# Column order batch by batch, and the even table one window earlier, in a DFT and squared-ReLU FFN kernel

## Chip, cores and metric

One NeuronCore of a Trainium2 chip. The metric is the device time of one execution in microseconds (us); less is better. The program is one core's alone, and there is no collective in it.

## What is computed

```
X = np.fft.fft(x, axis=1); X = np.fft.fft(X, axis=2)     # x: (8, 3008, 256) f32
t = X.real.reshape(8*3008, 256)
h = np.maximum(t @ w_in, 0.0)                            # w_in: (256, 2048)
out = h * h @ w_out                                      # w_out: (2048, 256), out: (24064, 256) f32
```

The kernel works in float16 with float32 accumulation in PSUM.

## The kernel before

**Columns.** A sequence row k of a batch and its mirror 3008 - k have transforms that differ only in the sign of one part. So the kernel works on *columns*: one column is the cosine part (`zc`) and the sine part (`zs`) of one row k, and it yields two output rows, "plus" and "minus". There are 1505 columns per batch, 12040 in all. A batch's columns come in two *units*: the odd unit (e = 0) with 752 columns, the even unit (e = 1) with 753. In each unit the first half of the columns is copied out of PSUM by ScalarE (L487) and the second half is made by VectorE from the same two accumulations (`minus`, L494).

**Order of the columns.** `units` (L86) lists the units in the order of their columns: before the change odd 0, odd 1, even 0, even 1, then odd i, even i for i = 2 to 7. (Numbers here are places in the order of work; batch 0 of the input is worked last.) The columns are cut into 25 *windows* (L73 to L78): w0 has 240 columns, w1 512, w2 and w3 376 each, w4 512, w5 448, then 512 each and 360 at the end. Unit odd 0 fills w0 and w1 exactly, odd 1 fills w2 and w3 exactly, even 0 begins at w4.

**What each window does** (L640 to L726). For each of 8 steps s, a window makes 256 of the 2048 hidden features for its columns: `pq` (L684, L685: four matmuls into PSUM, cosine and sine part), `square` with sign 0 (a ReLU by ScalarE from PSUM, L694, and a square by VectorE, L696, into `h2`), then `others(s)`, then `turn` (L690: two matmuls that turn plus into minus), and `square` with sign 1. `others(s)` holds all side work: first the list `at[s]`, then a share of the second FFN matmul of the *previous* window (L596, half groups of 8 matmuls, and their evacuation by ScalarE, L611, and stores on SP's queue, L576), then `post[s]`, then a share of the matmuls that make the columns of a later unit (`z_steps`, L478). In w0, w1 and w4 two steps are taken together (`ng` = 2): both `pq`, both squares, `others` of the first, both turns, both squares, `others` of the second.

**Buffers that tie the engines.** The PSUM tile `ph` has 2 buffers and `h1`, between ReLU and square, has 3. So TensorE can be at most two steps ahead of the ReLUs, and ScalarE at most three squares ahead of VectorE. Each engine works its queue strictly in the order of the program.

**Making a unit's columns.** For an odd unit `z_steps` issues 12 matmuls of 376 columns against the odd sine and cosine tables and the folded batch `od`. For an even unit it issues 20 matmuls of 188, 94 and 95 columns against the even tables `cos1`, `sin1` and the tiles `xt`, `yt`, `spn`. Between the first and the second half of each part ScalarE copies PSUM to `es` (L483). A unit that begins in window w+1 is made in window w (`need`), spread over steps `lo` to `hi` (L705 to L709), all at step 6 if `lo, hi = 6, 7`.

**Folding a batch** (`fold_steps`, L334). `d_even` (L348 to L350), `n_cos` (L358), `d_odd` (L353), `n_sin` (L361) and `odds` (L368) are VectorE work on the loaded batch `xo`; `nyq` (L373 to L375) is two tiny matmuls and a copy. `d_odd` also issues the load of the next batch, three to six DMAs on POOL's queue (L125, L130). `even` (L379) makes `ev` and writes it to a scratch in DRAM by a DMA of POOL's queue (L381); `back` reads it in four pieces, two by plain DMA (L389) and two by indirect DMA (L391), all on POOL's queue. `late` is four VectorE operations that read these pieces: two `fold8` (L404), two `fold16` (L415); behind the last come four tiny copies on POOL (`nyq8`, L421 to L423).

**The even table** (`table_steps(1)`): `freq` (L222, three operations), `args` (L232, two), `turns` (L236), `mods` (L242, two), `absm` (L245) and `weigh` (L265, four) on VectorE, `sins` (L248) and `coss` (L252) on ScalarE.

**The schedule before.** Ahead of w0: the odd table, odd half of fold 0, `gh` for all 2048 features, unit odd 0, then its two `minus` parts and `gh_turn(1)` to `gh_turn(3)` on VectorE (L543, L544, L558). In w0: `even` and `back` of batch 0 at step 2. In w1: fold 1 in steps 0 to 5 and unit odd 1 at step 6. In w2: `even` of batch 1, the even table, `late` of batch 0, `back` of batch 1. In w3: unit even 0. In w4: `late` of batch 1 in steps 0 to 3 and unit even 1 from step 4. From w5 on: fold 2, and so on in a steady pattern, a batch every three windows.

Of the kernel before, what the change touches and what calls it, by code (L numbers as in the profile page):

```python
# [19 lines left out]
def rev_dim(ap, i):  # L20

    dims = [list(d) for d in ap.ap]
    step, cnt = dims[i]
    dims[i] = [-step, cnt]
    return bass.AP(tensor=ap.tensor, offset=ap.offset + step * (cnt - 1), ap=dims)
# [3 lines left out]
def kernel(  # L29
# [15 lines left out]
    B, S, D = x.shape  # L45
    _, F = moe_w_in.shape
# [34 lines left out]
    def win_of(col):  # L81
        return max(w for w in range(NW) if wins[w][0] <= col) if col < TOT else NW


    bs = list(range(1, B)) + [0]
    units = [(0, 0), (1, 0), (0, 1), (1, 1)] + [(i, e) for i in range(2, B) for e in range(2)]  # L86
    runs = []
    col_of = {}
    g = 0
# [63 lines left out]
    def iota(shape, pattern, base, mult, name):  # L153
        t = const.tile(shape, I32, name=name)
        nc.gpsimd.iota(t, pattern=pattern, base=base, channel_multiplier=mult)
        return t
# [125 lines left out]
    at = const.tile([P, 2, P + 1], F32, name="at")  # L282
# [163 lines left out]
    def gh_turn(cc):  # L446
        f0 = cc * 512
        nc.vector.tensor_scalar(out=gh[:, 2, f0 : f0 + 512], in0=gh[:, 1, f0 : f0 + 512], scalar1=turn2[:, 0:1], scalar2=None, op0=ALU.mult)
# [3 lines left out]
    def zwin(w):  # L452
        if w not in zc:
            zc[w] = zp.tile([P, WN], F16, name="zc", tag="zc")
            zs[w] = zp.tile([P, WN], F16, name="zs", tag="zs")
        return zc[w], zs[w]
# [67 lines left out]
    def run(*jobs):  # L524
        for j in jobs:
            j()

    f0s = fold_steps(0)
    z0 = z_steps(need[0][0], late=True)
# [10 lines left out]
    gh_turn(0)  # L540
    gh3()
    run(*z0(1, 1))
    run(*z0(0, 2))  # L543
    run(*z0(1, 2))  # L544
    evec_i = iota([P, 2], [[1, 2]], 0, 2, "evec_i")

    evec = small([P, 2], "evec")
# [7 lines left out]
    nc.gpsimd.tensor_tensor(wge, wge, wg2, op=ALU.add)  # L555
    nc.gpsimd.tensor_scalar(out=wg2, in0=evec, scalar1=0.0, scalar2=-0.5, op0=ALU.is_equal, op1=ALU.mult)
    nc.gpsimd.tensor_tensor(wge, wge, wg2, op=ALU.add)
    for cc in range(1, F // 512):  # L558
        gh_turn(cc)

    def store(osb, p0, g0, m, minus, eng=nc.sync):

# [62 lines left out]
    def spread(jobs, i, n):  # L625
        return jobs[len(jobs) * i // n : len(jobs) * (i + 1) // n]

    folds = {0: f0s}

    def fold_jobs(i):  # L630
        f = folds[i] = fold_steps(i)
        return [f["d_even"], f["n_cos"], f["d_odd"], f["n_sin"], f["odds"], f["nyq"], f["even"], f["back"]]

    fold_at, late_at = {}, {}
    for i in range(2, B):
        fold_at[win_of(col_of[i, 0]) - 2] = i
        late_at[win_of(col_of[i, 1]) - 2] = i
    NST = NFC // 2
    old = None
    for w in range(NW):  # L640
        g0, wn = wins[w]
        h2 = h2p.tile([P, NFC, 2 * WN], F16, name="h2", tag="h2")
        zcw, zsw = zwin(w)

        lo, hi = 0, NST - 1
        at = [[] for _ in range(NST)]
        post = [[] for _ in range(NST)]
        if w == 0:
            at[2] = [f0s["even"], f0s["back"]]
        elif w == 1:  # L650
            fj = fold_jobs(1)
            at = [[f] for f in fj[0:5]] + [[], [], []]
            post[5] = fj[5:6]
            lo, hi = 6, 7
        elif w == 2:
            te = table_steps(1)
            at = [[folds[1]["even"], lambda: te["freq"](), lambda: te["args"](0)], [lambda: te["turns"](0)], [lambda: te["mods"](0)],
                  [lambda: te["absm"](0)], [lambda: te["sins"](0)], [lambda: te["coss"](0)], [], [lambda: te["weigh"]()]]
            for st in range(4):
                at[st + 3] = at[st + 3] + f0s["late"][st : st + 1]  # L660
            at[7].append(folds[1]["back"])
        elif w in fold_at:
            fj = fold_jobs(fold_at[w])
            at = [[f] for f in fj[0:5]] + [[], fj[6:7], fj[7:8]]
            post[5] = fj[5:6]
        elif w == win_of(col_of[1, 1]) - 1:
            for st in range(4):
                at[st] = folds[1]["late"][st : st + 1]
            lo = 4
        if w in late_at:  # L670
            for st in range(4):
                at[st + 2] = at[st + 2] + folds[late_at[w]]["late"][st : st + 1]
        zj, zl = [], []
        for u in need[w + 1]:
            zu = z_steps(u)
            zj += [(zu, 0, 0), (zu, 1, 0), (zu, 0, 1), (zu, 1, 1)]
        f2 = ffn2_steps(*old) if old else []
        phs = {}

        def pq(s):  # L680
            ph = phs[s] = ps_h.tile([P, 2, 512], F32, name="ph", tag="psh")
            for a in range(2):
                f0 = (2 * s + a) * P
                nc.tensor.matmul(ph[:, a, 0:wn], gh[:, 0, f0 : f0 + P], zcw[:, 0:wn], start=True, stop=False)  # L684
                nc.tensor.matmul(ph[:, a, 0:wn], gh[:, 1, f0 : f0 + P], zsw[:, 0:wn], start=False, stop=True)  # L685

        def turn(s):
            for a in range(2):
                f0 = (2 * s + a) * P
                nc.tensor.matmul(phs[s][:, a, 0:wn], gh[:, 2, f0 : f0 + P], zsw[:, 0:wn], start=False, stop=True, skip_group_check=True)  # L690

        def square(s, sg):
            h1 = h1p.tile([P, 2, 512], F16, name="h1", tag="h1")
            nc.scalar.activation(h1[:, :, 0:wn], phs[s][:, :, 0:wn], AF.Relu)  # L694
            hv = rev_dim(h1[:, :, 0:wn], 2) if sg else h1[:, :, 0:wn]
            nc.vector.tensor_tensor(h2[:, 2 * s : 2 * s + 2, sg * wn : (sg + 1) * wn], hv, hv, op=ALU.mult)  # L696

        def others(s):
            for j in at[s]:
                j()  # L700
            for j in spread(f2, s, NST):
                j()
            for j in post[s]:
                j()
            if s == lo:  # L705
                zl[:] = [j for zu, part, h in zj for j in zu(part, h)]
            if s >= lo:
                for j in spread(zl, s - lo, hi - lo) if s < hi else []:
                    j()  # L709


        ng = 2 if w == 0 or wins[w - 1][1] < 384 < wn else 1
        for s0 in range(0, NST, ng):
            ss = range(s0, s0 + ng)
            for s in ss:
                pq(s)
            for s in ss:
                square(s, 0)
            others(s0)
            for s in ss:  # L720
                turn(s)
            for s in ss:
                square(s, 1)
            for s in ss[1:]:
                others(s)
        old = (w, h2)  # L726
# [32 lines left out]
```

## Time and profile before

| what | us |
|---|---|
| median of 3 runs (634.8 to 634.96) | 634.92 |
| the profiled execution | 633.9 |
| its span, first to last instruction | 632.0 |
| TensorE busy | 615.9 |
| ScalarE busy | 457.4 |
| VectorE busy | 369.5 |
| POOL busy | 76.5 |

The page divides one profiled execution by engine, line and tile. "PE" is TensorE, "DVE" VectorE, "ACT" ScalarE, "POOL" GpSimd, "SP" the engine whose queue issues the stores. A line such as "L694" is a line of the kernel. An instruction's shown duration reaches into that of the next one where they are pipelined: eight matmuls of 256 columns at L596 are shown with 1.04 us, but the next work on TensorE begins 0.87 us after they began. What an instruction takes from its engine is the distance to the next start.

TensorE's first matmul of w0 starts at 21.73 us of the span, that of w1 at 31.68, of w2 at 53.20, of w3 at 74.81, of w4 at 94.54, of w5 at 116.98.

### The profile page before, as it was taken

How to read it: one execution, taken by the hardware profiler on the slowest of the kernel's cores; microseconds unless marked ns; L12 is line 12 of the kernel's file. 1: busy time of each engine (PE TensorE's matmuls, PEld its weight loads, DVE VectorE, ACT ScalarE, POOL GpSimd, SP SyncE). 2: the span in 40 equal slices, each digit the busy share in tenths (PEclk: the TensorE clock that was granted, in tenths of full speed). 3: DMA queues.
4: the chain of work that ended last, by engine and by line, in shares of the span. 5: the costliest groups of instructions: out<-in, count | busy, mean ns of one | idle time of the engine just before them, and what ended most of it. 6: DMA issues, size and time to landing. Idle time of an engine off the chain costs nothing.

```text
span 632.0 us, 11586 instructions
## 1 busy us (share of the span) xinstructions
PE 615.9 (97%) x4548; PEld 439.1 (69%) x4548; DVE 369.5 (58%) x604; ACT 457.4 (72%) x610; POOL 76.5 (12%) x125
## 2 busy tenths in 40 slices
PE   5899999999999999999999999999999999999997
PEld 2457776776777767767777677777677776777786
DVE  7887656765457557645576455854557555454430
ACT  7787778777777677767777777777777777777662
POOL 5352200022002200220011100030000200000000
PEclk9999999999999999999999999999999999999999
DMA  8936211172112711631127211262111311111112
GB/s 146 211 82 127 85 34 34 50 164 78 36 43 58 184 46 42 144 97 35 51 44 160 74 52 39 59 151 73 40 31 55 111 34 47 38 46 35 49 54 65
DMA packets 36525, 47.52 MB, mean 75 GB/s; under 512 B 4216, under 2 KB 30328, under 8 KB 36472
## 3 DMA queue, kind: packets, MB, share of 16 engines
q0 software_dynamic: 9344, 22.14, 17.6%
q1 hardware_dynamic: 26899, 24.44, 12.7%
q8 instruction: 35, 0.57, 0.4%
q10 hardware_dynamic: 228, 0.21, 0.1%
q14 instruction: 19, 0.15, 0.1%
HBM read 33.63 MB, written 27.84 MB: 97 GB/s over the span
## 4 chain that ended last, share of the span: by engine, by line
PE 93%; DVE 3%; ACT 2%; issue 1%; POOL 0%; ACTq 0%; POOLq 0%; DVEq 0%
PE po L596 51%; PE ph L684 12%; PE ph L685 12%; PE ph L690 12%; PE pz L478 4%; ACT h L694 1%; PE pw L301 1%; DVE h L696 1%; PE pg L436 0%; ACT cos L259 0%; DVE fe L349 0%; DVE fo L353 0%; ACT sin L248 0%; ACT gh L440 0%; DVE od L368 0%
## 5 line engine op out<-in xcount | busy, mean ns | idle before, releaser
L694 ACT ACTIVATE h<-ph 128x1024 f16<-128x1024 f32 (+4 forms) x400 | 368.4, 974 | 80.0 <-PE ph L690 72.1
L696 DVE TENSOR_TENSOR h<-h 128x1024 f16<-128x1024 f16 (+4 forms) x400 | 262.4, 660 | 231.6 <-ACT h L694 228.2
L596 PE MATMUL po<-wout,h 128*128 128x256 f16 (+1 forms) x3024 | 361.6, 273 | 0.0
L596 PEld LDWEIGHTS <-h 128*128 128x128 f16 (+1 forms) x3024 | 296.8, 98 | 71.3
L684 PE MATMUL ph<-zc,gh 128*128 128x512 f16 (+4 forms) x400 | 145.9, 366 | 1.1 <-ACT h L694 0.8
L685 PE MATMUL ph<-zs,gh 128*128 128x512 f16 (+4 forms) x400 | 145.9, 366 | 0.4 <-ACT zs L487 0.4
L690 PE MATMUL ph<-zs,gh 128*128 128x512 f16 (+4 forms) x400 | 112.8, 366 | 2.0 <-ACT h L694 1.5
L611 ACT ACTIVATE osb<-po 128x512 f32<-128x512 f32 (+3 forms) x95 | 54.9, 582 | 57.4 <-PE po L596 52.4
L685 PEld LDWEIGHTS <-gh 128*128 128x128 f16 x400 | 39.1, 98 | 43.8 <-issue 2.5
L684 PEld LDWEIGHTS <-gh 128*128 128x128 f16 x400 | 39.0, 98 | 41.8 <-issue 0.5
L690 PEld LDWEIGHTS <-gh 128*128 128x128 f16 x400 | 37.2, 97 | 12.7 <-issue 4.3
L421 POOL COPY xt<-xt 128x2 f16<-128x2 f16 x16 | 2.5, 186 | 173.2 <-DVE xt L404 173.2
L130 POOL DMA_INDIRECT xo<-in_x_dram,idx_r x15 | 22.1, 1471 | 4.6 <-issue 4.6
L125 POOL DMA_DIRECT2D xo<-in_x_dram x8 | 6.0, 751 | 109.8 <-DVE fo L353 109.8
L483 ACT ACTIVATE es<-pz 128x376 f32<-128x376 f32 (+1 forms) x32 | 15.4, 481 | 5.3 <-PE pz L478 5.2
L391 POOL DMA_INDIRECT rb<-scr,idx_r x16 | 18.5, 1158 | 4.9 <-issue 4.9
L487 ACT ACTIVATE zs<-pz 128x376 f16<-128x376 f32 (+23 forms) x27 | 8.5, 358 | 9.9 <-PE pz L478 9.9
L349 DVE TENSOR_TENSOR fe<-xo 128x3072 f16<-128x3072 f16 x8 | 14.3, 1786 | 1.6 <-DMA xo<-in_x_dram,idx_r 1.3
L353 DVE TENSOR_TENSOR fo<-xo 128x3072 f16<-128x3072 f16 x8 | 14.2, 1779 | 0.0
L494 DVE SCALAR_TENSOR_TENSOR zc<-es,pz 128x376 f16<-128x376 f32 (+20 forms) x26 | 9.4, 392 | 7.2 <-ACT zc L487 7.0
L301 PE MATMUL pw<-spn 128*128 128x384 f16 x30 | 8.2, 448 | 5.2 <-DVE spn L290 5.2
L389 POOL DMA_DIRECT2D rb<-scr x16 | 8.8, 551 | 33.4 <-DMA scr<-ev 33.0
(106 smaller groups left out, 220.4 us busy)
## 6 DMA issues: line engine op xcount, KB each, us to landing
out_dram<-osb SPq DMA_DIRECT2D x77, 128.0 KB
xo<-in_x_dram POOLq DMA_DIRECT2D x7, 768.0 KB, 7.0
scr<-ev POOLq DMA_DIRECT2D x8, 390.0 KB, 4.4
rb<-scr POOLq DMA_DIRECT2D x16, 130.0 KB, 5.1
out_dram<-osb SPq DMA_DIRECT2D x12, 94.0 KB
w<-in_moe_w_in_dram POOLq DMA_DIRECT2D x2, 512.0 KB, 10.0
wout<-in_moe_w_out_dram POOLq DMA_DIRECT2D x1, 1024.0 KB, 14.5
out_dram<-osb SPq DMA_DIRECT2D x8, 75.0 KB
```

What stands on the lines that cost most here:

```text
L130: nc.gpsimd.indirect_dma_start(out=flat(q), out_offset=None, in_=bass.AP(tensor=x.tensor, offset=0, ap=[[XW, B * S * D // XW], [1, XW]]), ...
L301: nc.tensor.matmul(pw[:, 0 : 3 * P], spn[:, 0, 0, :], spn.rearrange("p c r d -> p (c r d)")[:, 0 : 3 * P], start=True, stop=True)
L391: nc.gpsimd.indirect_dma_start(out=rb[:, q].rearrange("p r d -> p (r d)"), out_offset=None, in_=bass.AP(tensor=src.tensor, offset=src.offs ...
L478: nc.tensor.matmul(ps[:, o0:o1], lhs, tab, start=(h == 0 and k == 0), stop=last, skip_group_check=True)
L483: nc.scalar.activation(es[:, 0:n], ps[:, 0:n], AF.Copy, bias=0.0, scale=1.0)
L596: nc.tensor.matmul(po[0:m, j * D : (j + 1) * D], h2[:, fc, q : q + m], wout16[:, fc, :], start=(fc == 0), stop=(fc == NFC - 1))
L611: nc.scalar.activation(osb[0:mm].rearrange("p s d -> p (s d)")[:, lo:hi], po[0:mm, lo:hi], AF.Copy, bias=0.0, scale=HS * HS)
L684: nc.tensor.matmul(ph[:, a, 0:wn], gh[:, 0, f0 : f0 + P], zcw[:, 0:wn], start=True, stop=False)
L685: nc.tensor.matmul(ph[:, a, 0:wn], gh[:, 1, f0 : f0 + P], zsw[:, 0:wn], start=False, stop=True)
L690: nc.tensor.matmul(phs[s][:, a, 0:wn], gh[:, 2, f0 : f0 + P], zsw[:, 0:wn], start=False, stop=True, skip_group_check=True)
L694: nc.scalar.activation(h1[:, :, 0:wn], phs[s][:, :, 0:wn], AF.Relu)
L696: nc.vector.tensor_tensor(h2[:, 2 * s : 2 * s + 2, sg * wn : (sg + 1) * wn], hv, hv, op=ALU.mult)
```

## The change

The order of the units becomes odd 0, even 0, odd 1, even 1, odd 2 and so on, so even 0 takes columns 752 to 1504 (w2, w3 and one column of w4), and odd 1 columns 1505 to 2256 (w4, w5). With it the side work of the first windows is moved: the even table and `late` of batch 0 go from w2 to w1, unit even 0 is made at step 6 of w1, fold 1 goes from w1 to w2 (with `even` and `back` at steps 6 and 7), unit odd 1 from w1 to w3, `late` of batch 1 from w4 to steps 4 to 7 of w3, and unit even 1 is spread over all of w4. The three `gh_turn` and the two `minus` of unit odd 0 go from ahead of w0 into its steps 0, 2 and 4. No operation of the table, the folds or the FFN is added or taken away.

```diff
-    units = [(0, 0), (1, 0), (0, 1), (1, 1)] + [(i, e) for i in range(2, B) for e in range(2)]
+    units = [(i, e) for i in range(B) for e in range(2)]
...
     run(*z0(1, 1))
-    run(*z0(0, 2))
-    run(*z0(1, 2))
...
-    for cc in range(1, F // 512):
-        gh_turn(cc)
...
-    for i in range(2, B):
+    for i in range(1, B):
         fold_at[win_of(col_of[i, 0]) - 2] = i
         late_at[win_of(col_of[i, 1]) - 2] = i
...
         if w == 0:
-            at[2] = [f0s["even"], f0s["back"]]
+            at[0] = [lambda: gh_turn(1)]
+            at[2] = [lambda: gh_turn(2), f0s["even"], f0s["back"]]
+            at[4] = [lambda: gh_turn(3)] + z0(0, 2) + z0(1, 2)
         elif w == 1:
-            fj = fold_jobs(1)
-            at = [[f] for f in fj[0:5]] + [[], [], []]
-            post[5] = fj[5:6]
+            te = table_steps(1)
+            fl = f0s["late"]
+            at = [[lambda: te["freq"](), lambda: te["args"](0)], [lambda: te["turns"](0), lambda: te["mods"](0)], [lambda: te["absm"](0), lambda: te["sins"](0)],
+                  [lambda: te["coss"](0), fl[0]], [lambda: te["weigh"](), fl[1]], fl[2:4], [], []]
             lo, hi = 6, 7
-        elif w == 2:
-            te = table_steps(1)
-            at = [[folds[1]["even"], lambda: te["freq"](), lambda: te["args"](0)], [lambda: te["turns"](0)], [lambda: te["mods"](0)],
-                  [lambda: te["absm"](0)], [lambda: te["sins"](0)], [lambda: te["coss"](0)], [], [lambda: te["weigh"]()]]
-            for st in range(4):
-                at[st + 3] = at[st + 3] + f0s["late"][st : st + 1]
-            at[7].append(folds[1]["back"])
         elif w in fold_at:
             fj = fold_jobs(fold_at[w])
             at = [[f] for f in fj[0:5]] + [[], fj[6:7], fj[7:8]]
             post[5] = fj[5:6]
-        elif w == win_of(col_of[1, 1]) - 1:
-            for st in range(4):
-                at[st] = folds[1]["late"][st : st + 1]
-            lo = 4
-        if w in late_at:
+        if w in late_at:
+
             for st in range(4):
-                at[st + 2] = at[st + 2] + folds[late_at[w]]["late"][st : st + 1]
+                at[st + (4 if w == 3 else 2)] += folds[late_at[w]]["late"][st : st + 1]
```

## The prediction

> **What bounds the kernel now.** I read the page's busy shares first, then busy time by window, then the chain of waits through w1, then the timelines of the engines there.
>
> ```profile
> span 632.0 us, 11586 instructions
> PE 615.9 (97%) x4548; PEld 439.1 (69%) x4548; DVE 369.5 (58%) x604; ACT 457.4 (72%) x610; POOL 76.5 (12%) x125
> ```
>
> TensorE is busy all the time but 16 us. The windows (stretch, length, then busy time per engine) say where:
>
> ```profile
> 21.70:31.68 9.98, 7.46 (x51) 4.61 (x49) 8.78 (x22) 8.58 (x18) 2.18 (x8) 1.00 1.04 216
> 31.68:53.20 21.52, 19.95 (x127) 12.25 (x127) 17.08 (x27) 17.69 (x22) 11.66 (x7) 1.00 0.55 97
> 53.20:74.81 21.61, 21.61 (x178) 17.23 (x176) 15.73 (x34) 15.57 (x24) 2.90 (x8) 1.00 0.29 87
> 74.81:94.54 19.73, 19.66 (x167) 15.61 (x164) 10.51 (x23) 15.10 (x24) 1.66 (x2) 1.00 0.20 61
> 94.54:116.98 22.44, 22.19 (x166) 15.45 (x164) 13.88 (x24) 19.16 (x27) 0.70 (x4) 1.00 0.11 37
> ```
>
> w0 (first line) is bound by ScalarE and VectorE, TensorE idles 2.5 us. w1 idles 1.6 us of TensorE. w2 and w3 are bound by TensorE outright. The columns behind w4 keep their order and their work, so all that can change lies between 21.7 and 117 us. In w1 the chain of waits runs through fold 1 on VectorE:
>
> ```profile
> 35.56 1.79 DVE fe L349
> ...
> 38.63 0.88 DVE ab L358
> ...
> 40.72 1.70 DVE fo L353
> ...
> 43.60 0.88 DVE ab L361
> 44.49 1.20 DVE h L696 x2
> 45.69 0.90 DVE od L368
> 46.59 0.05 issue
> 46.63 0.18 PE py L373
> ```
>
> The squares queue between the folds, and `pq` of step 6 (46.70) stands behind `py`, which waits for `od`. Without any wait it would start at 31.68 + 3 pairs of steps x 4.34 (per pair 12 matmuls of 512 columns at 0.216 and two half groups of 8 at 0.872) = 44.70. So fold 1 costs w1 2.0 us, and that is what moving it could give back.
>
> **Method.** I walk the three queues by hand through w0 to w4, with starts to the next start from the timelines: ReLU 0.52 (240 columns), 0.92 (512), 0.69 (376); square 0.39, 0.60, 0.47; 0.2 from a matmul's issue end to ScalarE, 0.1 from ScalarE to VectorE or TensorE. For the kernel before this ends w1 at 53.11 (trace 53.20) and w4 at 116.64 (116.98): 0.1 per window is its error where it is applied to known work.
>
> **w0: +0.4.** Two `minus` (0.45 each) and three `gh_turn` (0.30 each) stand ahead of the first square now, and ScalarE pays for it once:
>
> ```profile
> 24.81 1.03 ACT L694 ACTIVATE h<-ph 128x480 f16<-128x480 f32 x2 [0.36 <-DVE h L696]
> ```
>
> That wait goes. But at step 4 the block `gh_turn(3)` and both `minus`, 0.30 + 2 x 0.48 = 1.26, stands between squares, and the ReLU of step 7 needs the `h1` buffer of the square behind it: a wait of 0.63. At step 2 `gh_turn(2)` goes ahead of `even` (0.89): 1.19 between squares, a wait of 0.39 where `even` alone made 0.09. Sum -0.54 (0.36 in the trace) + 0.63 + 0.30 = +0.39. Bounds: -0.36 if VectorE catches up, +0.6 with the trace's 0.36. I take +0.39. `even` itself starts where it did (26.9), since it follows the square of step 3.
>
> **w1: -0.48.** Out go fold 1 (VectorE 2.0 + 0.88 + 1.70 + 0.88 + 0.89 + 0.1 = 6.45) and 12 matmuls of 0.158. In come the table and `late` 0: VectorE 0.42 + 0.66 + 0.46 + 1.04 + 0.46 + 0.97 for the table, 2 x 0.61 + 2 x 0.34 for `late`, 5.9 in all, in smaller lumps. But ScalarE gets two operations that fold 1 did not have:
>
> ```profile
> 65.73 0.84 ACT L248 ACTIVATE sin<-m 128x754 f16<-128x754 f32 x1
> 68.28 0.93 ACT L252 ACTIVATE cos<-t,halfpi 128x754 f16<-128x754 f32 x1
> ```
>
> In w2 they lie beside 1.75 us of second FFN matmuls per step; in w1 a pair of steps gives TensorE 4.34 and ScalarE 4 x 0.92 + 0.5 (evacuation, every second pair) = 4.18 already. With 1.6 more in the second pair, ScalarE needs 5.8. Walked: `pq` of steps 2 and 3 from 36.4; `sins` waits for `mods` until 39.55; the ReLU of step 2, sign 1, ends at 41.3, so `pq` of step 4 waits 0.63; `coss` and the evacuation push the ReLU of step 4 to 43.5, so `turn` of steps 4 and 5 waits 0.52 and 0.49. `pq` of step 6 then starts at 46.73, the old 46.70: 1.64 of the 2.0 is spent again, the rest is w0's +0.39.
>
> The columns of even 0 are 20 short matmuls, 1.12 us of TensorE (0.08 per 188 columns, 0.04 per 94), against 1.90:
>
> ```profile
> 49.30 0.64 PE L478 MATMUL pz<-cos,od 128*128 128x376 f16 x3
> 49.77 0.64 PE L478 MATMUL pz<-sin,od 128*128 128x376 f16 x3
> 50.51 0.64 PE L478 MATMUL pz<-cos,od 128*128 128x376 f16 x3
> 50.99 0.64 PE L478 MATMUL pz<-sin,od 128*128 128x376 f16 x3
> ```
>
> All stand at step 6, so this gains nothing: TensorE waits for `es` (0.48 each) before the second halves, and after them ScalarE must make `zc`, `zs` (two spans each now, 0.18 for the one-column span) before the last ReLUs, for which w2's first `pq` waits until 53.02. `nyq8` on POOL follows the last `fold16` (49.5) by 0.45 as at 71.76 to 72.63, so `spn` is 0.15 late for its matmuls, inside the wait for `es`. w1 ends 0.1 earlier than before; less w0's +0.39 its own share is -0.48. Bounds: +1.3 (the whole of `sins` and `coss`, 1.77, on top of my -0.48), -2.0 (no wait at all).
>
> **w2: +0.07, w4: 0.** Fold 1 in w2 is laid out as fold 2 is from 119.4 on, where TensorE showed 10.00 of 10 us busy. It brings the load of batch 2 (POOL's queue, issued near 61 instead of 42.7; first read at 119.4, so its 7 to 11 us of landing are covered). Behind it on POOL's queue are the scratch write and four reads of batch 1; `even` 1 at 71.2, scratch landed 4 to 7.2 later, four issues 3.7, landing 3.8: 83 to 86. `late` 1 asks at 86.5; VectorE has 9 us idle in w3, and three squares of play. I charge nothing; uncovered it would cost up to 1. Four more stores in w0 to w7 (91 for 87) go to SP, whose 424 us of waiting for `osb` cover them.
>
> **w3: +0.53.** It gets the 12 long matmuls for the 20 short ones: +0.78 of TensorE work in a window where TensorE is busy 19.66 of 19.73. The small gaps before `turn` that the short ones leave take up 0.25. This is the work that w1 could not use.
>
> **Sum:** +0.39 - 0.48 + 0.07 + 0.53 = +0.5. The profiled execution becomes 633.9 + 0.5 = 634.4; the median stands 1.02 above it, so 635.4.
>
> **Rivals.** (A) *The even pieces come too late for w1.* `fold8` asks near 42.9 instead of 63.95; VectorE, ScalarE and TensorE would wait behind it. From the walk, a landing after 44.75 moves the end one for one. Before, the last piece was issued here:
>
> ```profile
> 34.34 1.05 POOL L391 DMA_INDIRECT rb<-scr,idx_r  x1 [0.30 <-issue]
> 35.69 2.50 POOL L391 DMA_INDIRECT rb<-scr,idx_r  x1 [0.30 <-issue]
> ...
> 43.79 4.84 POOL L130 DMA_INDIRECT xo<-in_x_dram,idx_r  x1 [0.30 <-issue]
> ```
>
> With 3.6 to 5.9 from issue to landing it landed by 39.3 to 41.6: three us of play. But an indirect issue took 4.84 beside fold 1's VectorE work. Two of these: 34.34 + 4.84 + 0.30 + 4.84 + 2.8 (shortest landing) = 47.1, which is 2.4 too late: 635.4 + 2.4 = 637.8. For it: the 2.50 beside `fe`, and squares run on. Against: the two `fe`, `fo` of 1.7 us are no longer there.
>
> The Trainium skill (DMA: Bandwidth & Descriptors, SWDGE vs HWDGE vs iDMA) says that GpSimd writes such descriptors into rings in SBUF and that VectorE shuts it out during its two-port modes. By that rule the table's float32 operations (L232, L236, L245) could hold these issues as `fe` may have done, and the time would be A's 637.8. The trace shows none of them beside an indirect DMA; the plain issue beside L222 and L232, at 57.02, took 0.75 where 0.61 is the median.
>
> (B) *w1 truly gains.* If `sins` and `coss` fit between ReLUs, `pq` of step 6 starts near 44.7: -2.0 in w1, and -0.36 in w0, against +0.53: -1.8, 633.1. For it: ScalarE idles 3.8 of 21.5 us in w1. Against: its idle time lies in waits for TensorE, with only two `ph` buffers to run ahead in. (C) *The moves do nothing*: table and even pieces are ready earlier, but ScalarE's chain sets the end of w1 as before (-0.1 with w0), and the 0.78 in w3 lies in gaps: 634.92 - 0.1 = 634.8. Against: w3 shows 0.07 of idle TensorE.
>
> **Chances.** What a measurement of this kernel can tell from no change is about 0.2%, 1.27 us. Forecast with C, within that: 0.69; own range 634.3 (w0's waits at -0.36, w1 0.35 better) to 636.2 (w0 at +0.6, w1 0.6 worse, a third of the way to its bound). A: 0.13, slower. The forecast with w0 and w1 at their worse bounds, +0.2 and +1.77: 637.4, slower, 0.09. B: 0.09, faster. Range 633.8 to 637.3: most of A, of the worst bounds and of B lies outside or at its ends, under 0.2 in all.
>
> **What would show it.** ScalarE's wait for a square at 24.8 gone, and new ones near 28 and 31; w1 starting near 32.0, `sins` near 39.6, `pq` of step 6 near 46.7, w2 near 53.0; w3 about 20.2 long; no DMA wait ahead of L404. Wrong if L404 waits for `rb`, if `pq` of step 6 comes before 45.5, or if a window from w5 on changes its length by more than 0.2.

## The result, and the profile after

The changed kernel took 635.68 us (median of 22 runs) against 634.07 us for the kernel before on the same chips: ratio 1.0025, 95% interval 1.0016 to 1.0034, some 1.6 us slower. In a second series, beside the experiments below, the ratio was 1.0017 (1.0007 to 1.0028). So it is slower, by about as much as the 0.2% that the prediction called its limit of sight, and inside the stated range; the forecast was +0.5 us. Both medians of "before" lie below the 634.92 that the prediction started from, which were three runs; the ratios compare runs of the same chips.

The profiled execution took 635.0 us with a span of 633.1 us (633.9 and 632.0 before). The windows again, first the changed kernel's w0 to w4 (stretch, length, then busy time of TensorE, its weight loads, VectorE, ScalarE and POOL):

```profile
21.56:31.67 10.11, 7.37 (x51) 4.61 (x48) 8.63 (x22) 8.52 (x18) 2.32 (x8) 1.00 1.01 212
31.67:54.17 22.50, 19.58 (x133) 12.37 (x133) 17.25 (x38) 18.83 (x26) 6.77 (x8) 1.00 0.13 37
54.17:75.83 21.66, 21.66 (x180) 17.27 (x178) 16.63 (x26) 14.04 (x22) 3.60 (x4) 1.00 0.58 129
75.83:96.09 20.26, 20.18 (x158) 15.46 (x156) 11.87 (x24) 15.14 (x24) 3.47 (x6) 1.00 0.25 76
96.09:118.52 22.43, 22.18 (x167) 15.45 (x164) 11.97 (x20) 19.38 (x27) 0.39 (x2) 1.00 0.11 33
```

| window | before, us | forecast change | measured change |
|---|---|---|---|
| w0 | 9.95 | +0.39 | +0.16 |
| w1 | 21.52 | -0.48 | +0.98 |
| w2 | 21.61 | +0.07 | +0.05 |
| w3 | 19.73 | +0.53 | +0.53 |
| w4 | 22.44 | 0 | -0.01 |
| sum | 95.25 | +0.51 | +1.71 |

w0 began 0.17 us earlier in this execution, which is chance (it began at 22.05 in the next run of the same kernel), so w5 begins 1.54 us later than before (118.52 against 116.98), and TensorE's last long row of matmuls likewise (618.35 against 616.81). The span grew by 1.1 only: what lies behind TensorE's last matmul, the last stores and the end of the program, took 0.4 us less. No run shows why.

Only w1 is far off. TensorE's waits in w1, by engine and line waited for (total, times, longest), first before:

```profile
PE py L373 <- DVE od L368: 1.0, 1, 1.0
PE ph L690 <- ACT h L694: 0.5, 1, 0.5
```

and after:

```profile
PE pz L478 <- POOL xt L421: 1.0, 1, 1.0
PE ph L673 <- ACT h L683: 1.0, 1, 1.0
PE ph L679 <- ACT h L683: 0.6, 2, 0.3
PE pz L478 <- ACT es L483: 0.3, 1, 0.3
```

The wait for fold 1 is gone, and the ScalarE waits came at the three places that the walk had named. The first line is new: the columns of even 0 wait for the four tiny POOL copies of `nyq8`. The timelines of the changed kernel show why (start, duration, engine, line; "x2" merges two instructions). POOL:

```profile
47.81 3.19 POOL L421 COPY xt<-xt 128x2 f16<-128x2 f16 x2 [11.14 <-DVE xt L404]
50.94 0.18 POOL L422 COPY spn<-yt 128x2 f16<-128x2 f16 x1
```

and VectorE beside it:

```profile
47.05 0.69 DVE L404 TENSOR_TENSOR xt<-rb 128x1040 f16<-128x1040 f16 x1
47.66 1.29 DVE L685 TENSOR_TENSOR h<-h 128x1024 f16<-128x1024 f16 x2
48.86 0.77 DVE L415 TENSOR_TENSOR yt<-xt 128x520 f16<-128x520 f16 x2
49.54 1.29 DVE L685 TENSOR_TENSOR h<-h 128x1024 f16<-128x1024 f16 x2
```

A copy of two elements per partition, 0.19 us at the median of its 16 instances (0.18 before, 0.19 at most), took 3.07 us here, the first of the two merged in that line. It begins under a square and ends as the sixth VectorE operation of an unbroken row ends (49.54 + 1.29 = 50.83). All six have two inputs in SBUF. The matmul that reads `xt` starts at 50.94, 0.99 late, and the `es` behind it adds 0.32.

### The profile page after: what moved, and what is told of

Its sections match the earlier page's. It is cut to its first block, busy times and chain, and to the rows that moved or that the text cites. A ratio compares the mean times of both kernels' runs of the same rounds, so it can differ in the third digit from the quotient of the medians.

```text
span 633.1 us, 11600 instructions
## 1 busy us (share of the span) xinstructions
PE 616.1 (97%) x4548; PEld 439.0 (69%) x4548; DVE 369.7 (58%) x606; ACT 457.1 (72%) x612; POOL 73.9 (12%) x125
## 4 chain that ended last, share of the span: by engine, by line
PE 91%; ACT 3%; DVE 2%; POOL 1%; DMA 1%; issue 1%; ACTq 0%; POOLq 0%; DVEq 0%
PE po L592 51%; PE ph L679 12%; PE ph L673 12%; PE ph L674 12%; PE pz L478 4%; ACT h L683 2%; DMA w<-in_moe_w_in_dram 1%; DVE h L685 1%; POOL xt L421 0%; PE pg L436 0%; POOL xo L130 0%; POOL perm L170 0%; DVE m L242 0%; ACT gh L440 0%; DVE t L232 0%
## 5 line engine op out<-in xcount | busy, mean ns | idle before, releaser
L421 POOL COPY xt<-xt 128x2 f16<-128x2 f16 x16 | 5.4, 368 | 160.3 <-DVE xt L404 160.3
L130 POOL DMA_INDIRECT xo<-in_x_dram,idx_r x15 | 18.1, 1205 | 4.6 <-issue 4.6
L391 POOL DMA_INDIRECT rb<-scr,idx_r x16 | 17.1, 1067 | 4.9 <-issue 4.9
L487 ACT ACTIVATE zs<-pz 128x376 f16<-128x376 f32 (+24 forms) x28 | 8.5, 348 | 10.3 <-PE pz L478 10.1
L494 DVE SCALAR_TENSOR_TENSOR zc<-es,pz 128x376 f16<-128x376 f32 (+22 forms) x27 | 9.4, 383 | 7.8 <-ACT zc L487 7.8
```

The lines of the kernel that those rows point to most:

```text
L130: nc.gpsimd.indirect_dma_start(out=flat(q), out_offset=None, in_=bass.AP(tensor=x.tensor, offset=0, ap=[[XW, B * S * D // XW], [1, XW]]), ...
L391: nc.gpsimd.indirect_dma_start(out=rb[:, q].rearrange("p r d -> p (r d)"), out_offset=None, in_=bass.AP(tensor=src.tensor, offset=src.offs ...
```

## The experiments

Two theories stood against each other. **Theory 1**: the missing microsecond is POOL's copies, held beside VectorE. **Theory 2**: ScalarE's chain sets the end of w1 in any case, and POOL's wait lies beside it. The three probes of POOL, the break, the tiny table and the short odd unit were run once each, and only their traces are read. Lengths of windows below are from the first matmul of one to the first of the next, in each run's own trace.

**The changed kernel again.**

> The changed kernel as it is, for the others to be compared with on one chip. Expected 1.5 us slower than the kernel before (TensorE's last matmul came 1.55 us later in the trace), ratio 1.0024; in its trace the first copy of L421 on POOL takes about 3 us and TensorE waits about 1.0 us for it at L478 in w1.

Measured: 635.46 us, ratio 1.0017 (1.0007 to 1.0028); w1 22.41, w3 20.27; TensorE waits 1.0 for POOL, with a copy of L421 held as before. The trace repeats to 0.1 us; the ratio is lower than expected, though its interval holds 1.0024.

**The copies on VectorE.**

```diff
-            xt, yt = st["xt"], st["yt"]
+            nyq_xt(nc.gpsimd)
+            nyq_spn(nc.gpsimd)
+
+        def nyq_xt(eng):
+            xt = st["xt"]
             for slot in range(2):
-                nc.gpsimd.tensor_copy(xt[:, 0, slot, :, 130:131], rev_dim(xt[:, 1, 1 - slot, :, 128:129], 1))
-            nc.gpsimd.tensor_copy(spn[:, 0, :, 0:1], yt[:, 1, 0, :, 128:129])
-            nc.gpsimd.tensor_copy(spn[:, 1, :, 0:1], yt[:, 0, 0, :, 128:129])
+                eng.tensor_copy(xt[:, 0, slot, :, 130:131], rev_dim(xt[:, 1, 1 - slot, :, 128:129], 1))
+
+        def nyq_spn(eng):
+            yt = st["yt"]
+            eng.tensor_copy(spn[:, 0, :, 0:1], yt[:, 1, 0, :, 128:129])
+            eng.tensor_copy(spn[:, 1, :, 0:1], yt[:, 0, 0, :, 128:129])
...
+        if i == 0:
+            late = [lambda: fold8(0), lambda: (fold8(1), nyq_xt(nc.vector)), lambda: fold16(0), lambda: (fold16(1), nyq_spn(nc.vector))]
```

> The changed kernel with batch 0's four tiny Nyquist copies (L421 to L423) on VectorE instead of POOL: the two of xt behind the second fold8, the two of spn behind the second fold16. Theory 1 (POOL's copies, held while VectorE works without a break, are the term that the forecast lacked): the wait of 0.99 for POOL and the 0.32 for es behind it shrink to about 0.3 in all, w1 gets 0.9 to 1.1 us shorter, and the kernel stands 0.4 to 0.6 above the kernel before (ratio about 1.0008). Theory 2 (ScalarE sets the end of w1, POOL's wait lies beside it): w1 gets less than 0.3 us shorter, ratio stays about 1.0022.

Measured: w1 21.46 (22.41 in the run beside it, -0.95), and nothing else moved; 634.39 us, ratio 1.0001 (0.9987 to 1.0014). The interval of the ratio overlaps that of the changed kernel; it is the window that decides. Theory 1 holds, theory 2 falls. The row of VectorE's operations shows what the copies cost there. From the `fold8` to the square are 0.88 us (47.21 to 48.09) where the changed kernel has 0.61, and from the `fold16` to the square 0.94 where it has 0.68, so 0.27 and 0.26 us:

```profile
47.94 0.24 DVE L425 COPY xt<-xt 128x2 f16<-128x2 f16 x2
48.09 1.28 DVE L694 TENSOR_TENSOR h<-h 128x1024 f16<-128x1024 f16 x2
49.29 0.76 DVE L415 TENSOR_TENSOR yt<-xt 128x520 f16<-128x520 f16 x2
50.09 0.17 DVE L429 COPY spn<-yt 128x2 f16<-128x2 f16 x1
50.16 0.16 DVE L430 COPY spn<-yt 128x2 f16<-128x2 f16 x1
50.23 1.28 DVE L694 TENSOR_TENSOR h<-h 128x1024 f16<-128x1024 f16 x2
```

**Part of the change alone, from both sides.** The `gh_turn` and `minus` taken back out of w0 (the lines below), and put into w0 of the kernel before (the same lines the other way round):

```diff
+    run(*z0(0, 2))
+    run(*z0(1, 2))
...
+    for cc in range(1, F // 512):
+        gh_turn(cc)
...
-            at[0] = [lambda: gh_turn(1)]
-            at[2] = [lambda: gh_turn(2), f0s["even"], f0s["back"]]
-            at[4] = [lambda: gh_turn(3)] + z0(0, 2) + z0(1, 2)
+            at[2] = [f0s["even"], f0s["back"]]
```

> The changed kernel with the three gh_turn and two minus parts put back ahead of w0. If moving them cost the 0.39 us that the forecast charged, w0 gets 0.4 us shorter; by the trace of the changed kernel it cost 0.15 (w0 10.11 against 9.95 us long), so 0.15 shorter. Theories 1 and 2 both leave the rest where it is: ratio 1.0020 to 1.0022.

> The kernel before with only the three gh_turn and two minus parts moved into w0, as the change has them. Forecast's charge: +0.39 us (ratio 1.0006); by the changed kernel's trace +0.15 (ratio 1.0002). A gain would mean that this part of the change is worth keeping by itself.

Measured: w0 is 9.93 in the first (10.11 with the change whole) and 10.10 in the second (9.95 before): 0.15 to 0.18 us either way, less than half of the 0.39. The times, 1.0013 (1.0002 to 1.0023) and 0.9991 (0.9980 to 1.0003), can't resolve it.

**A probe of POOL.** Three pairs of a memset and a copy on POOL in w1 of the kernel before, beside fold 1:

```diff
+    def probe():
+        for k in range(3):
+            nc.gpsimd.memset(pset[:, 2 * k : 2 * k + 2], 1.0)
+            nc.gpsimd.tensor_copy(pdst[:, 2 * k : 2 * k + 2], psrc[:, 2 * k : 2 * k + 2])
...
+            at[1] = [probe] + at[1]
```

> The kernel before with three pairs of a POOL memset and a POOL copy (128x2 f32, of no use to the output) put on POOL's queue at step 1 of w1, ahead of the next batch's load; they come up near 38 us, where VectorE works without a break (folds and squares, nearly all with two inputs). Theory 1: the memsets take about 0.1 us, the copies, which read SBUF, are held up to the next gap of VectorE or the next operation with one input, 0.5 to 4 us each. Rival (POOL's copies of L421 were slow for their strides or for their wait, not for VectorE): all six take 0.1 to 0.2 us.

POOL, and then VectorE beside it:

```profile
38.37 0.13 POOL L636 MEMSET pset<- 128x2 f32 x1
38.41 0.45 POOL L637 COPY pdst<-psrc 128x2 f32<-128x2 f32 x1
38.81 0.09 POOL L636 MEMSET pset<- 128x2 f32 x1
38.85 0.89 POOL L637 COPY pdst<-psrc 128x2 f32<-128x2 f32 x1
39.68 0.09 POOL L636 MEMSET pset<- 128x2 f32 x1
39.72 0.62 POOL L637 COPY pdst<-psrc 128x2 f32<-128x2 f32 x1
```

```profile
37.53 1.28 DVE L707 TENSOR_TENSOR h<-h 128x1024 f16<-128x1024 f16 x2
38.74 0.96 DVE L358 TENSOR_TENSOR ab<-fe 128x1560 f16<-128x1560 f16 x1
39.62 1.28 DVE L707 TENSOR_TENSOR h<-h 128x1024 f16<-128x1024 f16 x2
```

Beside the same operations the memsets run in 0.1 us, and the copies end 0.04 us after the VectorE operation that runs when they come up (38.86 after 38.81, 39.74 after 39.70). So what is held here is the POOL operation that reads SBUF, as theory 1 has it. But each was held by one operation, not by six.

**Whether the form of the copy matters.** The same probe with float16 copies, strided and reversed as those of L421 are; and two float32 copies ahead of L421 in the changed kernel:

```diff
+            if i == 0:
+                pdst = small([P, 2], "pdst")
+                nc.gpsimd.tensor_copy(pdst[:, 0:1], xt[:, 1, 0, 0, 128:130].bitcast(F32))
+                nc.gpsimd.tensor_copy(pdst[:, 1:2], xt[:, 1, 1, 0, 128:130].bitcast(F32))
```

> The kernel before with the same probe at step 1 of w1, but its three POOL copies are float16 with two strided, reversed elements per partition, as those of L421 are (the float32 ones took 0.45, 0.89 and 0.62 us, each to the end of one VectorE operation). If the form of the copy is what held L421 for 3 us, the first of these takes 2 us or more; if not, they take 0.4 to 0.9 us each like the float32 ones.

> The changed kernel with two float32 POOL copies of one element per partition (of no use to the output) that read the xt tile, ahead of batch 0's copies of L421. If any reading POOL copy is held there as long as VectorE works without a break, the first float32 copy takes about 3 us in their place and the two of L421 0.2 to 0.3; TensorE's wait for POOL in w1 is then 1.0 to 1.5 us. If the form of the L421 copies is the cause, the float32 copies take under 0.8 each and the first of L421 still ends near 50.9.

Measured: beside fold 1 the float16 copies took 0.45, 0.89 and 0.63 us, as the float32 ones had. Ahead of L421 the first float32 copy was held:

```profile
47.85 3.07 POOL L422 COPY pdst<-xt 128x1 f32<-128x1 f32 x1 [11.14 <-DVE xt L404]
50.87 0.17 POOL L423 COPY pdst<-xt 128x1 f32<-128x1 f32 x1
50.98 0.31 POOL L425 COPY xt<-xt 128x2 f16<-128x2 f16 x2
```

TensorE waited 1.2 us for POOL. So it is not the type or the form of the copy: the POOL copy that comes up first at 47.8 is held for 3.07 us. It need not be the place alone, though: the copies that were held long all read `xt`, and those beside fold 1 read a small tile that nothing else uses. No run has a copy of another tile at 47.8.

**A break in VectorE's row.**

```diff
+            brk = small([P, 2], "brk")
...
-... fl[1]], fl[2:4], [], []]
+... fl[1]], [fl[2], lambda: nc.vector.tensor_copy(brk, evec), fl[3]], [], []]
```

> The changed kernel with one VectorE copy of 128x2 float32 (one input, of no use to the output) between the two fold16 of batch 0. If POOL's copy is held by an unbroken row of VectorE operations with two inputs, it gets its turn at this copy, near 49.3: the first L421 copy takes about 1.5 us instead of 3.07, and TensorE's wait for POOL at L478 falls from 0.99 to under 0.2, w1 to about 21.5. If any VectorE work without an idle gap holds it, it still takes about 3 us.

The changed kernel with the break, POOL (both copies merged, then the first alone) and then VectorE:

```profile
48.51 3.14 POOL L421 COPY xt<-xt 128x2 f16<-128x2 f16 x2 [11.47 <-DVE xt L404]
48.51 1.54 POOL L421 COPY xt<-xt 128x2 f16<-128x2 f16 x1 [11.47 <-DVE xt L404]
```

```profile
49.56 0.43 DVE L415 TENSOR_TENSOR yt<-xt 128x520 f16<-128x520 f16 x1
49.90 0.17 DVE L653 COPY brk<-evec 128x2 f32<-128x2 f32 x1
49.98 0.42 DVE L415 TENSOR_TENSOR yt<-xt 128x520 f16<-128x520 f16 x1
50.31 1.28 DVE L686 TENSOR_TENSOR h<-h 128x1024 f16<-128x1024 f16 x2
```

Half right. The first copy got its turn at the break: it took 1.54 us and ended at 50.05, between the start and the end of the one-input operation (49.90 to 50.07). But the second then stood behind the next three two-input operations and took 1.66 us, the longest of L421 in this run. The pair still ended at 51.65, TensorE still waited 0.9 and w1 was 22.35. The expectation forgot that two copies need two turns.

**The table on ScalarE.** With the copies on VectorE, `sins` and `coss` for 8 of 377 columns (the rest of the table stays zero):

> The changed kernel with the copies on VectorE and with sins and coss of the even table made for 8 of 377 columns only (the rest of the table is zero, so the even rows are left out of the result): 1.76 us less of ScalarE in w1. Theory: sins and coss are what keeps w1 at 21.46 us; then the waits for the ReLU ahead of pq of step 4 and of turn of steps 4 and 5 go, and w1 is 1.2 to 1.8 us shorter, 19.7 to 20.3. Rival (VectorE's table and fold work sets the pace): w1 stays above 21.0.

Measured: w1 20.19 against 21.46, 1.27 us shorter. The two operations did not go to nothing, as the expectation reckoned: they are shown with 0.22 and 0.32 us where they took 0.83 and 0.92. So 1.2 us of ScalarE went, and all of it showed in w1. `sins` still began late, 0.55 us of waiting for `mods` on VectorE, which is part of what is left.

**The odd unit in w3.**

> The changed kernel with the copies on VectorE and 8 instead of 12 matmuls for unit odd 1 (a third of each of its sums is left out), 0.63 us less of TensorE in w3. If w3's 20.26 us (19.73 before) are the longer matmuls of the odd unit in a window that TensorE bounds, w3 is 19.65 to 19.75 long, and no other window changes. If late of batch 1, which the change puts in w3, made it longer, w3 stays near 20.2.

Measured: w3 19.88 against 20.26; the other windows keep their lengths within 0.12. The limits given were too low, since eight long matmuls are still 0.14 us more than the twenty short ones (8 x 0.158 against 1.12). TensorE's own starts settle it. From each matmul of L478 (the same line is L487 here) to the next start on TensorE, the unit's columns take 1.62 us of w3 before, 2.15 in the changed kernel and 1.76 with eight matmuls. The window has 19.73, 20.26 and 19.88 us: the same differences, to 0.01. So w3's growth is the longer matmuls, and `late` of batch 1 adds nothing to it.

**A version that beats both.** First the table spread over w0 and w1, then w0's VectorE blocks as well:

```diff
+    te = table_steps(1)
+    te["freq"]()
+    gh_turn(1)
...
-            at[0] = [lambda: gh_turn(1)]
-            at[2] = [lambda: gh_turn(2), f0s["even"], f0s["back"]]
-            at[4] = [lambda: gh_turn(3)] + z0(0, 2) + z0(1, 2)
+            at[0] = [lambda: gh_turn(2)]
+            at[2] = [f0s["even"], f0s["back"]]
+            at[4] = [lambda: gh_turn(3)] + z0(0, 2)
+            at[5] = z0(1, 2)
+            at[7] = [lambda: te["args"](0), lambda: te["turns"](0)]
...
-            at = [[lambda: te["freq"](), lambda: te["args"](0)], [lambda: te["turns"](0), lambda: te["mods"](0)], [lambda: te["absm"](0), lambda: te["sins"](0)],
-                  [lambda: te["coss"](0), fl[0]], [lambda: te["weigh"](), fl[1]], fl[2:4], [], []]
+            at = [[lambda: te["mods"](0)], [lambda: te["sin_row"](0), lambda: te["absm"](0)], [lambda: te["sin_row"](1)], [fl[0]],
+                  [lambda: te["cos_row"](0), lambda: te["wsin"](), fl[1]], [lambda: te["cos_row"](1), lambda: te["wcos"]()] + fl[2:4], [], []]
```

(The first version keeps the change's lines for steps 0, 2 and 4 of w0 and has no `gh_turn(1)` ahead; `sin_row`, `cos_row`, `wsin` and `wcos` are one row or one table of `sins`, `coss` and `weigh`. Both have the copies on VectorE.)

> A version meant to beat both: the changed kernel with the copies on VectorE, freq of the even table ahead of w0 (VectorE idles 0.78 there), args and turns at step 7 of w0 (VectorE idles 1.16 behind it), mods and absm in steps 0 and 1 of w1, and sins and coss one row at a time in steps 1, 2, 4 and 5, where ScalarE has 0.2 to 0.7 us to spare per pair of steps. If ScalarE's lump in the second pair of steps is what w1 waits for, w1 goes from 21.46 to 19.8 to 20.4, and the whole kernel lands 0.3 to 0.9 us below the kernel before (ratio 0.9987 to 0.9995). If VectorE sets the pace, w1 stays above 21.0 and the kernel at 1.0005 or more.

> table_split with w0's VectorE work spread too: gh_turn(1) behind freq ahead of w0, gh_turn(2) at step 0, even alone at step 2, gh_turn(3) and the first minus at step 4, the second minus at step 5. If the blocks of 1.2 us between squares are what makes ScalarE wait for a square in w0 (0.22 and 0.34), these waits go and w0 is 9.6 to 9.9 us long instead of 10.1, with w1 at 19.7 as before it; the whole then lies 1.3 to 1.5 us below the kernel before by TensorE's last matmul of w4 (ratio 0.9977 to 0.9985).

Measured: table_split has w1 at 19.70 and 633.14 us, ratio 0.9990 (0.9975 to 1.0004). The last version has 631.58 us, ratio 0.9963 (0.9951 to 0.9975), faster than the kernel before, and by more than was expected of it; w0 too is shorter than expected, 9.53 us. Its w0, w1 and w3:

```profile
21.71:31.24 9.53, 7.35 (x51) 4.61 (x48) 8.83 (x24) 8.47 (x18) 2.43 (x7) 1.00 1.07 224
31.24:50.94 19.70, 19.44 (x133) 12.32 (x133) 17.19 (x40) 18.68 (x28) 4.01 (x4) 1.00 0.14 43
...
72.60:92.87 20.27, 20.20 (x159) 15.46 (x157) 11.88 (x24) 15.15 (x24) 3.51 (x6) 1.00 0.26 75
```

ScalarE is busy 18.68 of 19.70 us in w1, where the changed kernel took 22.50 us for the same ScalarE work; TensorE's waits there are 0.2 us in all. By the trace w0 to w4 take 93.58 us, 1.67 less than before; the ratio says 2.3 (1.6 to 3.1).

## Why the prediction came out as it did

**What was right.** The place: all the difference lies in w0 to w4, TensorE shows no wait from w5 on. w3's +0.53 came to the hundredth, and with it the reason that the change could not gain much: 0.78 us of TensorE work left a window where ScalarE set the pace for one where TensorE does. w2 and w4 came within 0.02. In w1 fold 1's waits went, and the lump of `sins` and `coss` gave them back as three ReLU waits. Measured as the walk counts, by the distance of TensorE's starts less its work, they are 1.14, 0.48 and 0.49 us for the 0.63, 0.52 and 0.49 of the walk (the views show 0.97, 0.32 and 0.32 of idle time).

**What was luck.** The median of 635.68 stands so near the 635.4 of the forecast because the walk's base, 634.92, lay 0.85 above the 634.07 that 22 runs of the kernel before gave; the change itself was +1.6 for +0.5. And `sins` and the `pq` of step 6 start in the trace near the forecast 39.6 and 46.7 (39.71, 46.85) only since w1 began at 31.67 and not at 32.07; counted from the start of w1 both are half a microsecond late.

**The term that was mis-sized** is w1's: -0.48 forecast, +0.98 measured. It has two parts, one behind the `pq` of step 6 and one ahead of it.

The larger, 0.95 us by the run with the copies on VectorE, is the step that took `nyq8` from its row at 71.76 to 72.63: "`nyq8` on POOL follows the last `fold16` (49.5) by 0.45 as at 71.76 to 72.63, so `spn` is 0.15 late for its matmuls, inside the wait for `es`". The row was right for its place, w2, where VectorE idles between squares (1.29 us ahead of the squares at 70.61). At step 5 of w1 VectorE has a row of six operations without a gap, and the copies were held, first one of `xt`, of which the prediction says nothing. From the `pq` of step 6 to the end of w1 are 7.32 us (46.85 to 54.17), where the walk had 6.37 (46.73 to 53.10) and the run with the copies on VectorE 6.38.

The smaller, some 0.5 us, is VectorE's table. `freq` to `mods` were charged 0.42 + 0.66 + 0.46 + 1.04 = 2.58; in the changed kernel they run from 35.31 to 39.59 with two squares of 0.60 between, so 3.08. So `sins` began 8.04 us into w1 and not 7.48, and the first ReLU wait grew from 0.63 to 1.14. `freq` was read too short (its three operations take 0.59 from start to next start in the trace of before, too), and `args` took 0.86 for 0.66, `turns` 0.58 for 0.46.

**w0** was over-charged, +0.39 for +0.16: the waits came at the two places named, but as 0.28 and 0.39 us, not 0.39 and 0.63 (ScalarE's distance from start to start less the walk's 0.52 for a ReLU; shown as 0.23 and 0.34 of idle time). The wait that went had been 0.41 in this count, not 0.54. Both single-part runs agree with the 0.16.

**Rival A**, the late pieces, did not come: the last indirect issue took 0.98 us at 35.69, where it had taken 2.50 beside fold 1, and no `fold8` of batch 0 or 1 waited for a DMA. The table's float32 operations, which the prediction feared, did not hold it: L222 and L232 ran beside it (35.31 to 36.77). But it was the right worry in the wrong place: what VectorE shut out here was a POOL copy. **Rival B**, a true gain, was refused by the order of ScalarE's work and not by its amount: with the same ScalarE operations spread over w1, and `freq`, `args` and `turns` on VectorE done ahead of it, w1 takes 19.70 us. **Rival C** falls with w3.

## What to carry to other kernels

A profile row for a small operation on POOL holds for its neighbourhood only: before moving one, look at what VectorE does beside it. Where VectorE's row has no gaps, try it on VectorE; here 0.53 us there bought 0.95 of the window. When a window changes its bound from one engine to another, ask where the first engine's work went: work that leaves a window which another engine paces is saved there by nobody, and is paid in full where it arrives. And an engine that idles 3.7 us in a window, as ScalarE does in w1, can still set its end; what counts is whether each lump fits between two waits.

## What the runs showed of the hardware

In these traces POOL copies that read SBUF waited for VectorE operations with two inputs in SBUF, whatever the copy's type: they took 0.45 to 0.89 us each behind one operation, while memsets between them took 0.1. That agrees with the Trainium skill (SBUF — State Buffer, Who interferes with whom), by which such a VectorE instruction contends with a GpSimd instruction that reads SBUF and not with one that only writes it.

The Trainium skill (SBUF — State Buffer, SBUF: two separate sides) says that whichever of the two starts first has the shared ports for its whole instruction, and that the other blocks. Here it was more: in an unbroken row of six VectorE operations POOL's copy was passed over five times and took 3.07 us, in both traces of the changed kernel, in that with the turns ahead of w0, and again with another copy in front. A one-input VectorE operation in the row let the first copy in after 1.54 us; the second was then passed over twice and took 1.66. Beside fold 1, in a row that shows no gaps either, copies got their turn after one operation. Whether the row or the tile that the copy reads makes this difference was not tried and stays open.

One input does not make every VectorE operation harmless. In the last version a POOL operation (L573) that begins with a `gh_turn`, which has one input, took 0.39 us where its like in the same run took 0.23 to 0.24, and in the run with the short odd unit another (L560) took 0.37.
